# One MLP unit back from the Strassen form, attention's weighted sum as one strided reduction, and DVE work handed to GpSimd, in a two-layer attention and MLP kernel

## The chip, the cores and the metric

The kernel runs on one core of a Trainium2 chip. The metric is the device time in microseconds (us) of one execution. The engines are named as in the profile: PE is the matrix engine, DVE the vector engine, ACT the scalar engine, POOL is GpSimd, SP is the engine that issues most DMAs. Each engine runs its own queue of instructions in the order in which they were written, and waits at the head of its queue until what an instruction needs is there.

## The reference

Two layers follow each other twice on 2048 tokens of 640 numbers in fp32: sliding attention, then an MLP, each with a layernorm ahead and a residual sum behind.

```python
S, D, H, Dh, W, dil, F = 2048, 640, 32, 20, 8, 2, 1536
def A(x, wqkv, wo):
    q, k, v = heads(x @ wqkv)                     # 32 heads of 20
    # token s sees the tokens s, s-2, ..., s-14, those below 0 masked
    logits = einsum("bhsd,bhswd->bhsw", q, k[idx]) * Dh ** -0.5
    o = einsum("bhsw,bhswd->bhsd", softmax(logits), v[idx])
    return merge(o) @ wo
def B(y, w1, b1, w2, b2):
    return gelu(y @ w1 + b1) @ w2 + b2
for _ in range(2):
    x = x + A(layernorm(x), wqkv, wo)
    x = x + B(layernorm(x), w1, b1, w2, b2)
```

## The kernel before

The tokens of each parity are independent in attention, so the 2048 tokens are cut into four units of 512 (two parities, two halves), and the two layers make eight unit steps, numbered 0 to 7. In a unit each of the 128 partitions holds four consecutive tokens of its parity.

Matrix products are made in split form: a fp32 operand is written as a high and a low fp16 half, and three products (high with high, high with low, low with high) are summed, so a product over 640 takes 15 matmuls.

A unit step goes as follows. `layernorm` (ACT, with the power -0.5 on POOL, L487) writes y, its two halves and, by a DMA transpose, `yT`. `qkv` projects (L539), ACT evacuates to `ev`, and `put` stores q, k and v to a scratch tensor in HBM (`spill`), from ACT's queue. `fetch` loads them back with the seven tokens ahead of each partition's own. `attention` then works on one group of 8 heads (160 numbers per token) at a time, four groups per unit, 32 groups `G` in all. For each half of a group (two tokens per partition) DVE multiplies q by the eight shifted k (L606), sums over the 20 numbers of a head (L610), takes the softmax over 8 terms (L618 to L625; L618 and L623 reduce over the shifts, which lie 8 floats apart), multiplies by the shifted v (L632, into `pr`, laid out as token, shift, 160 numbers), and adds the eight shifts in three additions of halves: eight to four and four to two (L640), two to one (L644, into `o`). ACT writes the high half of `o` to `ohl`, DVE the low half (L653). `project` transposes `ohl` by DMA (4 times per unit) and multiplies by wo (L672); DVE adds to the residual x (L678).

A unit's plain MLP (`mlp`) runs 12 steps: 15 matmuls to 128 hidden columns (L709), gelu and high half on ACT (L715, L718), low half on DVE (L720), and 24 matmuls into the accumulators (L728, L731), at the end DVE's residuals (L751). For the units in `FAST_OUT`, `mlp_fast` does the second product in a Strassen-like form, with seven products in place of eight: sums of hidden blocks (L854, on POOL except for unit 7), their halves (L849) and 252 matmuls of 320 columns (L900). The weight sums for it are made by `prep_sums` (30 operations on POOL, L776) and kept in HBM. Behind the layernorm of the MLP, b2 is added to x (L515).

The order of all engines' queues is worked out ahead by `Plan`: every operation is added with an engine, an estimated duration and a priority; `run` simulates the engines and starts, at each point, the operation that can start first, ties by priority, with buffers taken from pools. The code is then written out in that order, so a queue's order is fixed before the kernel runs, and an operation that takes longer than estimated delays what stands behind it.

```python
for w in (4, 2):
    dve(EH * w * GC, G - 0.9, lambda vk=vk, w=w: nc.vector.tensor_add(
        tile_of(*vk)[:, :, 0:w], tile_of(*vk)[:, :, 0:w], tile_of(*vk)[:, :, w:2 * w]),
```

Of the kernel before, what the change touches and what calls it, by code (L numbers as in the profile page):

```python
# [15 lines left out]
P = 128  # L16
KD = D // P
NF = F // P
NG = 4
# [27 lines left out]
FAST_OUT = (6, 7)  # L47
# [16 lines left out]
class Plan:  # L64
# [12 lines left out]

    PATIENCE = 0.7
# [12 lines left out]
    def add(self, eng, dur, prio, emit, need=(), give=(), use=(), table=None, move=0.0, lazy=False):  # L91
        o = dict(eng=eng, dur=dur, prio=prio, emit=emit, need=need, give=give, use=use, table=table,
                 move=move, lazy=lazy, n=len(self.ops))
# [6 lines left out]
    def run(self):  # L100
# [13 lines left out]
        order = []  # L114

        def start(o):
# [3 lines left out]
            for k in o["need"]:  # L120
                e, w = when[k]
                w = w + (self.LAG[e] if e != o["eng"] else 0.06 * (e != "pe"))
                t = max(t, w)
            new = {}
            for u in o["use"]:
                if u in self.slot:
                    t = max(t, self.since[u])
                else:
# [7 lines left out]
                    new[u[0]] = i + 1  # L136
            return t

        total = len(self.ops)
        while len(order) < total:  # L140
# [19 lines left out]
            d = o["dur"]  # L160
            if o["table"] and o["table"] != table:
                table = o["table"]
                d += self.SWITCH
# [21 lines left out]
            for k in o["give"]:  # L185
                when[k] = (e, end)
# [19 lines left out]
def sliding_dilated_then_mlp_kernel(  # L206
# [76 lines left out]
    T["g"] = [b[:, :NS * HT2].rearrange("p (s c) -> p s c", s=NS) for b in (act_buf, ev_buf)]  # L283
# [27 lines left out]
    def dve(n, prio, emit, need=(), give=(), use=(), more=0.0):  # L311
        plan.add("dve", v_cost(n) + more, prio, emit, need, give, use)
# [3 lines left out]

    def dma(kb, prio, emit, need=(), give=(), use=(), by="sp"):
        lazy = give[0][0] in ("x", "sq", "st", "c1", "c2", "zero", "mw", "tr", "ms", "fw") or give[0] in ("b1", "b2")
        plan.add(by, 0.1 if by == "act" else 0.38, prio, emit, need, give, use, move=kb / 330.0, lazy=lazy)

    def dma_transpose(prio, emit, need=(), give=(), use=()):
        plan.add("sp", 1.45, prio, emit, need, give, use, move=1.4)
# [5 lines left out]
    def constants():  # L328
        nc.vector.memset(half, -0.5)
# [6 lines left out]
    def mask_value():  # L336
        nc.vector.tensor_scalar(mask, mask, 0.0, -1e9 / scale, op0=OP.is_lt, op1=OP.mult)
# [67 lines left out]
    def prep_m(f, i, prio):  # L405
# [4 lines left out]
        dma(328, prio - 5, lambda: nc.scalar.dma_start(mw[i][f], tile_of(*ck)),  # L410
            need=[("lo", ("m", f, i))], give=[("mw", f, i)], use=[ck], by="act")

    def turn(prio, t, name, hk, yk):

        for a in range(2):
# [10 lines left out]
            def copy(a=a, turned=turned):  # L426
                to = transposed(yk)[:, a * KD:(a + 1) * KD, t * P:(t + 1) * P]
                ps = turned().rearrange("p (k c) -> p k c", k=KD)
                if a:
                    nc.vector.tensor_copy(to, ps)  # L430
# [12 lines left out]
    def layernorm(n, prio, yk, twice):  # L443
# [13 lines left out]
        for t in range(m if fast else 0):  # L457
            def stats(t=t):
# [3 lines left out]
                nc.vector.tensor_scalar_add(bn[:, t, 13:14], bn[:, t, 13:14], EPS)  # L462
# [19 lines left out]
        for t0 in range(0, 0 if fast else m, cut):  # L482
# [4 lines left out]
            pool(2.5, prio, lambda t0=t0, t1=t1: nc.gpsimd.tensor_tensor(  # L487
# [6 lines left out]
        for t in range(m):  # L494
# [19 lines left out]
            if twice:  # L514
                dve(D, -350, lambda t=t: nc.vector.tensor_add(x[u][:, t], x[u][:, t], b2),  # L515
                    need=[("y", name, t), ("fg", n, 2, 0) if n in FAST_OUT else ("hhi", at(n, t) * NF + 2 * t + 2), "b2"], give=[("xb", n, t)])

# [3 lines left out]
    def qkv(n):  # L521
# [6 lines left out]
        for k, (g, b) in enumerate(halves):  # L528
            ek = ("ev", (n, g, b))
            for i in range(2):  # L530
# [12 lines left out]
                mm(3 * KD * 3 * GC, 15, -500 + n + 0.01 * k, product,  # L543
# [5 lines left out]
            def put(g=g, b=b, ek=ek):  # L549
                to = spill[la][par]  # L550
                nc.scalar.dma_start(
# [5 lines left out]
                give=[("put", n, g, b)], use=[ek], by="act")  # L557
# [20 lines left out]
    def attention(G):  # L578
# [21 lines left out]
        for a in range(NE):  # L600
# [3 lines left out]
            def qk(t0=t0, pk=pk):  # L604
                w = tile_of(*wk)
                nc.vector.tensor_mul(tile_of(*pk), w[:, HALO + m + t0:HALO + m + t0 + EH, None, :].to_broadcast([P, EH, W, GC]),  # L606
# [5 lines left out]
                axis=AX.X, op=OP.add), need=[("qk", G, a)], give=[("lg", G, a)], use=[pk, sk])  # L612
# [14 lines left out]
        for a in range(NE):  # L627
# [3 lines left out]
            def pv(t0=t0, vk=vk):  # L631
                nc.vector.tensor_mul(  # L632
# [5 lines left out]
            last = ("pv", G, a)  # L638
            for w in (4, 2):
                dve(EH * w * GC, G - 0.9, lambda vk=vk, w=w: nc.vector.tensor_add(  # L640
                    tile_of(*vk)[:, :, 0:w], tile_of(*vk)[:, :, 0:w], tile_of(*vk)[:, :, w:2 * w]),
                    need=[last], give=[("ad", G, a, w)], use=[vk])
                last = ("ad", G, a, w)
# [356 lines left out]
```

## Time and profile before

| what | value |
|---|---|
| median of 2 runs | 1189.59 us (1188.9 to 1190.28) |
| the profiled execution's own time | 1189.57 us |
| its span | 1187.8 us |
| mean granted clock of PE | 0.99 |
| last attention result written | 1052.47 us |

The span runs from the first to the last instruction; the execution's time is 1.8 us longer. A group's row in the profile names line, engine, operation, the program's tensors, the shape (partitions x elements) and the count, then busy time and mean duration of one, then the time its engine sat idle just before.

### The profile page before, as it was taken

What the parts mean: (1) busy time and instruction counts of PE and PEld (TensorE: products, weight loads), DVE (VectorE), ACT (ScalarE), POOL (GpSimd) and SP (SyncE); (2) the same over time, 40 slices, a digit from 0 to 9 for tenths busy, and PEclk for the clock granted to TensorE, in tenths of its full rate; (3) what the DMA queues carried; (4) which work ended last, traced back from release to release, by engine and by line L of the source; (5) the groups of instructions that cost most, each with busy time, mean ns of one, the idle gap of its engine ahead of it and who ended that gap; (6) DMA issues with size and microseconds to landing.
All of it is one profiled execution on the core that took longest, in us unless ns stands there. A gap on an engine that the chain in (4) does not pass through costs nothing.

```text
span 1187.8 us, 17373 instructions
## 1 busy us (share of the span) xinstructions
PE 1153.7 (97%) x6844; PEld 632.0 (53%) x6844; DVE 1063.6 (90%) x1030; ACT 538.3 (45%) x939; POOL 153.0 (13%) x100
## 2 busy tenths in 40 slices
PE   7999999999979999999999999999998799989998
PEld 4444446577544565545554455546454555447556
DVE  7899999999999999999998999989999999873361
ACT  6476444535283435732637253364343552344240
POOL 1011000001010000000002010022055440450000
PEclk9999999999999999999999999999999899989999
DMA  9998999889675558577565757568766894546645
GB/s 303 289 314 271 309 328 279 244 264 289 172 218 161 175 170 205 164 195 207 153 199 150 203 152 210 182 159 175 212 237 238 231 241 130 183 100 187 182 124 173
DMA packets 235758, 248.77 MB, mean 209 GB/s; under 512 B 131148, under 2 KB 185756, under 8 KB 235676
## 3 DMA queue, kind: packets, MB, share of 16 engines
q1 hardware_dynamic: 206620, 208.34, 61.5%
q10 hardware_dynamic: 29056, 39.33, 9.5%
q8 instruction: 53, 0.87, 0.3%
q14 instruction: 29, 0.24, 0.1%
HBM read 168.76 MB, written 48.71 MB: 183 GB/s over the span
## 4 chain that ended last, share of the span: by engine, by line
PE 66%; DVE 21%; issue 6%; POOL 3%; ACT 2%; DMA 2%; SPq 0%; DVEq 0%; POOLq 0%; ACTq 0%
PE ps L539 25%; PE ps L709 12%; PE acc L728 9%; PE ps L672 8%; PE acc L900 6%; DVE pr L606 4%; DVE pr L632 4%; PE ps L834 3%; DVE pr L640 3%; DVE sm L610 3%; PE acc L731 2%; POOL ln L487 2%; DVE act L720 2%; DVE xf L515 1%; DVE hl L506 1%
## 5 line engine op out<-in xcount | busy, mean ns | idle before, releaser
L539 PE MATMUL ps<-wq,yT 128*128 128x480 f16 x1920 | 392.6, 367 | 0.0
L539 PEld LDWEIGHTS <-yT 128*128 128x128 f16 x1920 | 187.9, 98 | 201.2 <-issue 1.5
L709 PE MATMUL ps<-yT,c 128*128 128x512 f16 (+1 forms) x1260 | 248.8, 351 | 6.4 <-DMA yT<-hl 6.4
L728 PE MATMUL acc<-c,act 128*128 128x512 f16 x864 | 240.4, 379 | 2.4 <-DVE act L720 2.3
L632 DVE TENSOR_TENSOR pr<-sm,v 128x2560 f32<-128x2560 f32 x64 | 182.4, 2868 | 0.0
L709 PEld LDWEIGHTS <-c 128*128 128x128 f16 x1260 | 120.7, 98 | 114.7 <-issue 9.9
L606 DVE TENSOR_TENSOR pr<-qk 128x2560 f32<-128x2560 f32 x64 | 179.6, 2807 | 0.1
L610 DVE TENSOR_REDUCE sm<-pr 128x128 f32<-128x2560 f32 x64 | 179.6, 2806 | 0.0
L731 PE MATMUL acc<-c,act 128*128 128x128 f16 x864 | 178.6, 219 | 0.9 <-DVE act L720 0.9
L487 POOL TENSOR_TENSOR ln<-ln,half 128x2 f32<-128x2 f32 (+1 forms) x30 | 58.2, 1938 | 761.1 <-ACT ln L484 761.1
L672 PE MATMUL ps<-wo,yT 128*128 128x320 f16 x960 | 136.7, 305 | 14.2 <-DMA yT<-ohl 12.4
L545 ACT ACTIVATE ev<-ps 128x480 f32<-128x480 f32 x128 | 72.3, 566 | 170.3 <-PE ps L539 169.9
L640 DVE TENSOR_TENSOR pr<-pr 128x640 f32<-128x640 f32 (+1 forms) x128 | 148.7, 1184 | 0.0
L728 PEld LDWEIGHTS <-act 128*128 128x128 f16 x864 | 84.2, 98 | 101.0 <-DVE act L720 3.7
L672 PEld LDWEIGHTS <-yT 128*128 128x128 f16 x960 | 95.4, 100 | 55.9 <-DMA yT<-ohl 14.2
L715 ACT ACTIVATE act<-ps,b 128x512 f32<-128x512 f32 (+1 forms) x84 | 52.1, 623 | 156.4 <-PE ps L709 148.1
L731 PEld LDWEIGHTS <-act 128*128 128x128 f16 x864 | 82.0, 98 | 8.9 <-DVE act L720 1.0
L834 PE MATMUL ps<-yT,c 128*128 128x512 f16 x360 | 78.5, 379 | 0.4 <-ACT act L840 0.3
L470 ACT ACTIVATE junk<-xf 128x640 f16<-128x640 f32 x56 | 41.2, 735 | 81.6 <-DVE xf L678 71.4
L720 DVE TENSOR_TENSOR act<-act 128x512 f16<-128x512 f32 (+1 forms) x84 | 58.0, 693 | 15.2 <-ACT act L718 15.1
L776 POOL TENSOR_TENSOR wq<-wq 128x320 f32<-128x320 f32 (+1 forms) x30 | 56.4, 1898 | 67.8 <-ACT wq L798 47.4
L900 PE MATMUL acc<-c,wq 128*128 128x320 f16 x420 | 61.8, 299 | 0.0
(82 smaller groups left out, 942.0 us busy)
## 6 DMA issues: line engine op xcount, KB each, us to landing
c<-mw SPq DMA_DIRECT2D x192, 320.0 KB, 3.4
spill<-ev ACTq DMA_DIRECT2D x64, 480.0 KB, 4.2
qk<-spill SPq DMA_DIRECT2D x32, 880.0 KB, 6.2
v<-spill SPq DMA_DIRECT2D x32, 880.0 KB, 4.9
qk<-spill SPq DMA_DIRECT2D x32, 320.0 KB, 4.0
mw<-c ACTq DMA_DIRECT2D x24, 320.0 KB, 4.7
c<-msp SPq DMA_DIRECT2D x24, 320.0 KB, 3.5
act<-in_B_w_dram SPq DMA_DIRECT2D x21, 320.0 KB, 5.6
```

The lines of the kernel that those rows point to most:

```text
L487: pool(2.5, prio, lambda t0=t0, t1=t1: nc.gpsimd.tensor_tensor(col(2)[:, t0:t1], col(2)[:, t0:t1], half[:, t0:t1], op=OP.pow), need=[("vr" ...
L539: nc.tensor.matmul(ps, transposed(yk)[:, a * KD + k, t * P:(t + 1) * P], wq[:, b, k, g], start=j == 0, stop=j == 3 * KD - 1)
L606: nc.vector.tensor_mul(tile_of(*pk), w[:, HALO + m + t0:HALO + m + t0 + EH, None, :].to_broadcast([P, EH, W, GC]), windows(w, t0, [GC, W], ...
L610: dve(E, G - 0.7, lambda pk=pk, t0=t0: nc.vector.tensor_reduce(lg(t0, t0 + EH).rearrange("p t w h -> p (t w h)"), tile_of(*pk).rearrange(" ...
L632: nc.vector.tensor_mul(tile_of(*vk).rearrange("p t w (h d) -> p t (w h) d", d=DH), lg(t0, t0 + EH).rearrange("p t w h -> p t (w h)")[:, :, ...
L640: dve(EH * w * GC, G - 0.9, lambda vk=vk, w=w: nc.vector.tensor_add(tile_of(*vk)[:, :, 0:w], tile_of(*vk)[:, :, 0:w], tile_of(*vk)[:, :, w ...
L672: nc.tensor.matmul(tile_of(*pk)[:, :D // 2], transposed(yk)[:, a * KD + k, t * P:(t + 1) * P], wo[:, b, k, c * D // 2:(c + 1) * D // 2], s ...
L709: nc.tensor.matmul(tile_of(*pk)[:, :nt], tile_of(*ck)[:, a, k * P:(k + 1) * P], transposed(yk)[:, c * KD + k, t0 * P:t1 * P], start=i == 0 ...
L728: nc.tensor.matmul(acc[i], w, tile_of(*wk)[:, c, :BANK], start=e == 0 and (a, c) == PASS[0], stop=end, skip_group_check=True)
L731: nc.tensor.matmul(acc[4][:, i * P:(i + 1) * P], w, tile_of(*wk)[:, c, BANK:], start=e == 0 and i == t0 and (a, c) == PASS[0], stop=end, s ...
L834: nc.tensor.matmul(tile_of(*pk), tile_of(*ck)[:, a, k * P:(k + 1) * P], transposed(yk)[:, c * KD + k, :], start=i == 0, stop=i == 3 * KD - 1)
L900: nc.tensor.matmul(acc[bank][:, :HD], tile_of(*hk)[half][:, a, slot, t * P:(t + 1) * P], load()[:, z, c], start=q in FIRST and i == 0 and ...
```

## The change

It has several parts.

- `FAST_OUT` goes from (6, 7) to (7,): unit 6's MLP is computed in plain form, unit 7's keeps the Strassen form. The two buffers of the Strassen form's sums change places, and their wait for the unit ahead moves from its first to its second step.
- Attention's three additions become one `tensor_reduce` that reads `pr` with the shift as innermost dimension, 160 floats from term to term, and writes `o`.
- The low half of `o` (three groups of four) and the addition of b2 (units 0 to 6) are done by POOL (`laid`). A DVE operation can be marked with `opens`; while it runs, a window is open in the plan in which such a POOL operation can be placed. The POOL operation is then made to wait for the DVE instruction ahead of the one that opens the window.
- `prep_sums` moves from POOL to DVE, at a low priority.
- The stores of q, k and v and of the split MLP weights go from ACT's queue to SP's.
- The plan adds spare time (0.5 us for a DMA, 2.0 for a transpose) to what PE waits for from DMA, and counts 3.0 instead of 2.5 us for the power on POOL. Unit 4's projection gets a later priority.

```diff
-FAST_OUT = (6, 7)
+SPARE = (0.5, 2.0)
+FAST_OUT = (7,)
...
+        def window(o, t):
+            for w in windows:
+                if o["beside"] > w[3]:
+                    continue
+                s = max(t, w[0])
+                if s + o["dur"] <= w[1] + self.OVER:
+                    return s, w
+            return None, None
...
-                e, w = when[k]
-                w = w + (self.LAG[e] if e != o["eng"] else 0.06 * (e != "pe"))
+                e, w, spare = when[k]
+                w = w + (self.LAG[e] if e != o["eng"] else 0.06 * (e != "pe")) + spare * (o["eng"] == "pe")
...
-    T["g"] = [b[:, :NS * HT2].rearrange("p (s c) -> p s c", s=NS) for b in (act_buf, ev_buf)]
+    T["g"] = [b[:, :NS * HT2].rearrange("p (s c) -> p s c", s=NS) for b in (ev_buf, act_buf)]
...
+    def laid(n, prio, emit, until, need=(), give=(), use=(), level=1):
+        plan.add("pool", 0.17 + n / 450.0, prio, emit, need, give, use, beside=level, until=until)
...
-                dve(D, -350, lambda t=t: nc.vector.tensor_add(x[u][:, t], x[u][:, t], b2),
-                    need=[("y", name, t), ("fg", n, 2, 0) if n in FAST_OUT else ("hhi", at(n, t) * NF + 2 * t + 2), "b2"], give=[("xb", n, t)])
+                last = lambda by, t=t: by.tensor_tensor(x[u][:, t], x[u][:, t], b2, op=OP.add)
+                if n in FAST_OUT:
+                    dve(D, -350, lambda last=last: last(nc.vector), need=[("y", name, t), ("fg", n, 2, 0), "b2"], give=[("xb", n, t)])
+                else:
+                    laid(D, -250 + n, lambda last=last: last(nc.gpsimd), lambda ready, when, k=("rest", n, PARTS[at(n, t)][1]): k in when, need=[("y", name, t), "b2"], give=[("xb", n, t)], level=2)
...
-                nc.scalar.dma_start(
+                nc.sync.dma_start(
...
-            last = ("pv", G, a)
-            for w in (4, 2):
-                dve(EH * w * GC, G - 0.9, lambda vk=vk, w=w: nc.vector.tensor_add(
-                    tile_of(*vk)[:, :, 0:w], tile_of(*vk)[:, :, 0:w], tile_of(*vk)[:, :, w:2 * w]),
-                    need=[last], give=[("ad", G, a, w)], use=[vk])
-                last = ("ad", G, a, w)
-            dve(EH * GC, G - 0.9, lambda vk=vk, t0=t0: nc.vector.tensor_add(
-                tile_of(*ok)[:, t0:t0 + EH], tile_of(*vk)[:, :, 0], tile_of(*vk)[:, :, 1]),
-                need=[last], give=[("o", G, a)], use=[vk, ok])
+            dve(E, G - 0.9, lambda vk=vk, t0=t0: nc.vector.tensor_reduce(
+                tile_of(*ok)[:, t0:t0 + EH], tile_of(*vk).rearrange("p t w c -> p t c w"), axis=AX.X, op=OP.add),
+                need=[("pv", G, a)], give=[("o", G, a)], use=[vk, ok], opens=2)
...
+        low = lambda by: by.tensor_tensor(tile_of(*hk)[:, :, 1, g * GC:(g + 1) * GC], tile_of(*ok), hi(), op=OP.subtract)
+        if g < NG - 1:
+            laid(m * GC, -300 + G, lambda: low(nc.gpsimd), lambda ready, when: any(("o", G + 1) in q["use"] for q in ready.get("dve", ())), need=[("oh", G)], give=[("ol", G)], use=[ok, hk])
+        else:
+            dve(m * GC, -300 + G, lambda: low(nc.vector), need=[("oh", G)], give=[("ol", G)], use=[ok, hk])
...
-            pool(1.0, prio, f, need=need, give=[("ts", j, name)], use=[key])
+            dve(HD, prio, f, need=need, give=[("ts", j, name)], use=[key])
...
+        if o["behind"]:
+            tc.add_manual_dep(o["ins"].ins, o["behind"]["ins"].ins.name, mybir.DependencyInfo(
+                mybir.DependencyClass.Sync, mybir.DependencyReason.DATA), reason="order")
```

The order of the queues changes throughout. At the end of the last attention group DVE's queue stands like this before (`pr` holds the weighted values, `o` the sums, `wq` the halves of unit 6's Strassen sums; a number behind a name is the buffer's):

```order
L640 TENSOR_TENSOR pr_74<-pr_74 128x2x640
L640 TENSOR_TENSOR pr_75<-pr_75 128x2x640
L849 TENSOR_TENSOR wq<-ev,wq 128x768
L849 TENSOR_TENSOR wq<-ev,wq 128x1024
L515 TENSOR_TENSOR xf<-xf,b_103 128x640 x4
L849 TENSOR_TENSOR wq<-act,wq 128x768
L849 TENSOR_TENSOR wq<-act,wq 128x1024
L640 TENSOR_TENSOR pr_74<-pr_74 128x2x320
L640 TENSOR_TENSOR pr_75<-pr_75 128x2x320
L644 TENSOR_TENSOR o_86<-pr_74 128x320
L644 TENSOR_TENSOR o_86<-pr_75 128x320
L653 TENSOR_TENSOR ohl_73<-o_86,ohl_73 128x4x160
```

And like this now, with L668 the product, L674 the reduction, L753 the low half of the plain MLP and L809 the weight sums:

```order
L668 TENSOR_TENSOR pr_75<-sm_88,v_69 128x2560
L753 TENSOR_TENSOR act<-act 128x512
L674 TENSOR_REDUCE o_86<-pr_75 128x320
L753 TENSOR_TENSOR act<-act 128x512
L668 TENSOR_TENSOR pr_74<-sm_88,v_69 128x2560
L809 TENSOR_TENSOR wq<-wq 128x4x320
L753 TENSOR_TENSOR act<-act 128x512
L674 TENSOR_REDUCE o_86<-pr_74 128x320
L809 TENSOR_TENSOR wq<-wq 128x4x320
L683 TENSOR_TENSOR ohl_73<-o_86,ohl_73 128x4x160
```

The six additions have become two reductions, b2 and the Strassen halves have left this place, and one weight sum has come ahead of the last reduction.

On PE, at the last matmul of the last output projection (`wo` is its weight), this followed before:

```order
L672 LDWEIGHTS yT_72
L672 MATMUL ps_94<-wo,yT_72 128x320
L900 LDWEIGHTS wq
L900 MATMUL acc_95<-c_76,wq 128x320
L900 LDWEIGHTS wq
```

Now this follows, with L705 the projection and L761 and L764 the plain MLP's second product:

```order
L705 MATMUL ps_94<-wo,yT_71 128x320
L761 LDWEIGHTS act
L761 MATMUL acc_97<-c_79,act 128x512
L764 LDWEIGHTS act
L764 MATMUL acc_99<-c_79,act 128x128
```

Where unit 6's 252 Strassen products stood behind the projection, 407 matmuls of unit 6's plain MLP stand now, ahead of unit 7's MLP in both.

POOL's queue early in the program held nothing but the powers of the layernorms (`ln`), after those of the first two (`bn`):

```order
L465 TENSOR_TENSOR bn<-bn,half 128x1 x8
L487 TENSOR_TENSOR ln_91<-ln_91,half 128x2 x2
L487 TENSOR_TENSOR ln_89<-ln_89,half 128x2 x2
L487 TENSOR_TENSOR ln_90<-ln_90,half 128x1 x4
L487 TENSOR_TENSOR ln_91<-ln_91,half 128x2
```

Now the low halves (L683) and the additions of b2 (L548, on `xf`) stand between them:

```order
L498 TENSOR_TENSOR bn<-bn,half 128x1 x8
L520 TENSOR_TENSOR ln_91<-ln_91,half 128x2 x2
L520 TENSOR_TENSOR ln_89<-ln_89,half 128x2 x2
L683 TENSOR_TENSOR ohl_73<-o_86,ohl_73 128x4x160 x3
L520 TENSOR_TENSOR ln_90<-ln_90,half 128x1 x4
L548 TENSOR_TENSOR xf<-xf,b_103 128x640
L683 TENSOR_TENSOR ohl_73<-o_86,ohl_73 128x4x160
```

A power that stands behind one of these waits until it has run.

More of the change, by code (lines that the diff above doesn't have):

```diff
@@ L114, in run @@
         order = []
+        windows = []
+        shut = sum(o["opens"] > 0 for o in self.ops)
+        ahead = None
+        def window(o, t):
[6 more added lines that the diff above has]
+            return None, None
         def start(o):
@@ L136, in start @@
                     new[u[0]] = i + 1
+            if o["beside"] and (shut or windows):
+                s, _ = window(o, t)
+                return s if s is not None or shut and not o["until"](ready, when) else t
             return t
@@ L185, in run @@
             for k in o["give"]:
-                when[k] = (e, end)
+                when[k] = (e, end, o["spare"])
                 for w in waiting.pop(k, ()):
@@ L328, in constants @@
     def constants():
[L329 removed]
+        return nc.vector.memset(half, -0.5)
     dve(8, -900, constants, give=["half"])
@@ L823, in mlp_fast @@
             gk, hk = ("g", (b, jj)), ("h", (b, jj))
+            if jj == 1:
+                free += [("out", b - 1, NF - 1, i) for i in range(M)]
             for s in range(2):
```

80 lines of the change are left out of this document (45 added, 35 removed).

## The prediction

> **What bounds the kernel now.** I read the page's busy shares and slices first, then the table of stretches, then the groups of VectorE (DVE) by shape, and last the chain of waits near the end.
>
> ```profile
> span 1187.8 us, 17373 instructions
> PE 1153.7 (97%) x6844; PEld 632.0 (53%) x6844; DVE 1063.6 (90%) x1030; ACT 538.3 (45%) x939; POOL 153.0 (13%) x100
> PE   7999999999979999999999999999998799989998
> DVE  7899999999999999999998999989999999873361
> ```
>
> Two engines are nearly full. PE is full to the end; DVE is full for some 34 of 40 slices and falls off when attention is over. So the table of stretches is cut where the last attention result is written (1052.47 us), and, in a second answer, into pieces of the time before.
>
> ```profile
> 0.00:1052.47 1052.47, 1026.12 (x6035) 552.21 (x6036) 1009.66 (x943) 498.09 (x876) 143.99 (x90) 0.99 0.73 215
> 1052.47:1057.62 5.15, 1.26 (x6) 0.39 (x5) 4.35 (x4) 3.79 (x5) 2.63 (x3) 0.84 0.49 93
> 1057.62:1187.80 130.18, 126.36 (x804) 79.44 (x804) 49.62 (x84) 36.42 (x58) 6.40 (x8) 0.98 0.59 166
> ...
> 0.00:15.00 15.00, 10.01 (x91) 7.24 (x92) 8.56 (x21) 5.22 (x6) 2.15 (x11) 0.89 0.94 295
> 15.00:100.00 85.00, 84.04 (x436) 41.18 (x434) 78.42 (x91) 56.09 (x111) 13.08 (x10) 1.00 0.92 285
> 800.00:900.00 100.00, 98.58 (x571) 52.20 (x570) 99.45 (x82) 42.03 (x71) 30.86 (x17) 1.00 0.72 202
> 900.00:1000.00 100.00, 91.30 (x558) 49.44 (x557) 100.00 (x88) 47.64 (x73) 35.22 (x18) 0.97 0.77 229
> ```
>
> The columns are the stretch, its length, then busy time of PE, weight load, DVE, ACT and POOL. Up to the last attention result DVE is busy 1009.7 of 1052.5 us: it idles 42.8 us, 13.0 of them in the first 100 us, and between 800 and 1000 us 0.6 us, while PE idles 10. From there to the end stand 5.15 us of storing and transposing and 130.2 us in which PE has 126.4 us of work. So the end is the time of the last attention result, set by DVE's sum, plus the PE work that stands in PE's order behind the last output projection. DVE had no more than about 30 us to spare after the start. An edit that adds to attention on DVE shows almost fully; one that takes from it soon meets PE.
>
> **The strided sum.** These are DVE's groups by shape (busy us, mean ns of one):
>
> ```profile
> L610 DVE TENSOR_REDUCE sm<-pr 128x128 f32<-128x2560 f32 x64 | 179.6, 2806 | 0.0
> L640 DVE TENSOR_TENSOR pr<-pr 128x1280 f32<-128x1280 f32 x64 | 96.4, 1521 | 0.0
> L640 DVE TENSOR_TENSOR pr<-pr 128x640 f32<-128x640 f32 x64 | 53.5, 846 | 0.0
> L720 DVE TENSOR_TENSOR act<-act 128x512 f16<-128x512 f32 x60 | 48.2, 804 | 14.0 <-ACT act L718 13.9
> L644 DVE TENSOR_TENSOR o<-pr 128x320 f32<-128x320 f32 x64 | 32.7, 521 | 0.0
> L515 DVE TENSOR_TENSOR xf<-xf,b 128x640 f32<-128x640 f32 x32 | 29.2, 925 | 0.0
> L653 DVE TENSOR_TENSOR ohl<-o,ohl 128x640 f16<-128x640 f32 x32 | 27.6, 862 | 3.0 <-ACT ohl L651 3.0
> L618 DVE TENSOR_REDUCE sm<-sm 128x32 f32<-128x256 f32 x32 | 19.5, 608 | 0.0
> L751 DVE SCALAR_TENSOR_TENSOR xf<-acc,xf 128x512 f32<-128x512 f32 x29 | 18.3, 681 | 1.0 <-PE acc L731 0.9
> L619 DVE TENSOR_TENSOR sm<-sm 128x256 f32<-128x256 f32 x32 | 13.3, 416 | 0.0
> L849 DVE TENSOR_TENSOR wq<-act,wq 128x1024 f16<-128x1024 f32 x6 | 7.3, 1223 | 5.5 <-ACT wq L851 5.5
> ```
>
> Consecutive operations overlap a little, so the timeline gives the step from start to start:
>
> ```profile
> 110.16 1.47 DVE L640 TENSOR_TENSOR pr<-pr 128x1280 f32<-128x1280 f32 x1
> 111.56 2.81 DVE L632 TENSOR_TENSOR pr<-sm,v 128x2560 f32<-128x2560 f32 x1
> ...
> 119.80 0.61 DVE L618 TENSOR_REDUCE sm<-sm 128x32 f32<-128x256 f32 x1
> 120.33 2.81 DVE L606 TENSOR_TENSOR pr<-qk 128x2560 f32<-128x2560 f32 x1
> ```
>
> The 1.47 us addition is followed after 1.40: a step is its duration less 0.07. The three additions cost (1.521+0.846+0.521) - 3*0.07 = 2.68 us, 64 times 171.4 us. In their place stand 64 reductions over 2560 elements, whose price R is not in the trace. At the low end, L610 reduces 2560 elements that lie side by side: 2.74 us a step. But the new one reads its eight terms 640 bytes apart (160 floats). The trace has one reduction that reads with a gap: L618 takes groups of eight terms 32 bytes apart, and 256 elements cost 608 ns where L619 passes 256 in 416. The excess, 192 ns, is 0.75 ns per element, so 2560 elements would take 2.74 + 1.92 = 4.66 us. Read by its step, 0.53 us for 256, ten times as many cost 5.3; by its full duration, 6.08 - 0.07 = 6.0. L618 is the nearest row, in kind of operation, group length and gap, so I stay with it, between its first two readings: R = 5.0, with 2.74 and 6.0 as far ends. The additions were 171.4; the reductions are 320.
>
> The Trainium skill says otherwise in "VectorE: DVE Perf Modes", Mode 1x (REGULAR): one result per cycle with no assumption on the pattern ("fp32, weird strides, PSUM operands — all work"). By that rule the sum would be near that of L610, the first rival below. The L618 row speaks against it; another page, "SBUF — State Buffer", Door 1: The DMA port swizzle, has each access that enters a new 16-byte line pay a penalty, which agrees with L618's excess and would scale it by the element.
>
> **What leaves and joins DVE before the last attention result.** The low halves of the attention output go to POOL for three groups in four: 24 x (0.862-0.07) = 19.0 us off. Adding b2 goes to POOL for units 0 to 6: 28 x (0.925-0.07) = 23.9 off. Unit 6 in plain form takes six splittings of L849 away (6 x 1.15 = 6.9), five residuals of L751 (5 x 0.61 = 3.1) move behind the last result and one more L720 (0.7) ahead of it: 9.3 off. Of the 30 weight sums that come from POOL, eight of 320 and one of 1280 elements stand ahead: 8 x 0.45 + 1.45 = 5.1 on. Together, without R: -171.4 - 19.0 - 23.9 - 9.3 + 5.1 = -218.5. With 64 x 5.0 = 320 DVE gains 101.5 us of work, and has 1111.2 ahead of the last result.
>
> **POOL.** What it takes over is priced by its uncontended runs:
>
> ```profile
> 861.47 3.45 POOL L776 TENSOR_TENSOR wq<-wq 128x320 f32<-128x320 f32 x4 [31.50 <-ACT wq L798]
> 873.64 5.79 POOL L776 TENSOR_TENSOR wq<-wq 128x320 f32<-128x320 f32 x4 [2.34 <-ACT wq L798]
> 961.85 2.62 POOL L776 TENSOR_TENSOR wq<-wq 128x1280 f16<-128x1280 f32 x1 [1.38 <-ACT wq L803]
> ```
>
> 0.86 us for 320 elements and 2.62 for 1280 give 1.45 for 640; 52 of them are 75 us on an engine that is 13% busy and sheds the weight sums. I cost them at nothing; what hides them is the long reductions, behind whose predecessor each is made to wait. If that cover goes, they cost DVE up to 75 (second rival). Behind each stand POOL's layernorm powers, and behind those PE; with DVE setting the pace PE has room.
>
> **PE.** The chain of waits shows the prices:
>
> ```profile
> 394.76 3.24 PE ps L709 x15
> 401.26 3.24 PE ps L709 x15
> ...
> 1057.62 18.98 PE ps L672 x120
> ...
> 1149.76 34.24 PE acc L900 x252
> ```
>
> A step of the plain MLP takes 6.50 us and a unit twelve: 78.0. The Strassen form takes 12 x 3.24 + 34.24 = 73.1. PE's sum grows by 4.9 us. Of more weight is the order: behind the last projection PE had unit 6's 252 Strassen products and unit 7, and now has 407 of unit 6's plain matmuls (39 to a step, so 10.4 steps, 67.8 us) and unit 7. The end lies 5.15 + 130.2 - 34.2 + 67.8 = 168.9 us behind the last attention result, against 135.3.
>
> **Queues.** 64 stores of q, k, v and 24 of split weights go from ACT's queue to SP's, behind what SP waits for:
>
> ```profile
> spill<-ev ACTq DMA_DIRECT2D x64, 480.0 KB, 4.2
> mw<-c ACTq DMA_DIRECT2D x24, 320.0 KB, 4.7
> ...
> SPq L570 <- DVE pr L632: 137.7, 26, 11.0
> ```
>
> SP's longest such wait is 11.0 us. Unit 0's stores come before any such wait and later units are projected well ahead, so I take nothing, at most 11, and see no gain over 4.2 x 2 at the start. Unit 4's later projection and the swapped buffers only reorder PE work with slack: nothing, within the idle time below.
>
> **The sum.** DVE's idle time before the last result was 42.8 us: 13.0 at the start stays; of the rest I keep half (800 to 1000 us shows that it vanishes where DVE binds), 28 in all, ends 13 and 43. 1111.2 + 28 + 168.9 = 1308.1 us of span. The profiled run took 1189.57 us, 1.8 over its span, and the median of the runs is 1189.59: 1310. With R from 4.66 to 5.3 and idle time from 13 to 43 this goes from 1273 to 1344.
>
> **Rivals.** *The gap costs nothing on DVE* (R = 2.74, or an excess per instruction: 2.93). DVE's path is then 1009.7 - 43.1 + 28 + 168.9 + 1.8 = 1165, and PE decides: 1189.6 + 4.9 = 1194.5, less what it waited for and may no longer:
>
> ```profile
> PE ps L672 <- DMA yT<-ohl: 12.4, 3, 6.8
> PE ps L709 <- DMA yT<-hl: 6.4, 1, 6.4
> ```
>
> That is 1176 to 1195; 1187 within 2%. It ends on the other side. For it speaks L610; against it L618. It decides as long as R stays under 2.74 + (1213.4-1165)/64 = 3.5 us. *POOL blocks DVE*: R small, but the 52 moved operations each hold up DVE for 1.45: 1165 + 75 = 1240. For it: the same four POOL operations took 3.45 and 5.79 us, and L515 averages 925 ns where L640's form of 640 elements takes 846. Against it: each starts behind a named instruction ahead of a reduction. It needs 33 of 52 to pass 2%. *The gap costs more than L618's*: R = 6.0 gives 1374.
>
> **Chances.** The forecast (R 4.4 to 5.6) 0.72; the gap free 0.18; POOL blocking or an R between 0.05; R over 5.6 0.05. Of the free case 0.02 is faster by over 2% and 0.16 within; of the 0.05 for POOL or an R between, 0.01 falls within too. So faster 0.02, same 0.17, slower 0.81; 2% (24 us) is about what a measurement of this kernel can tell from no change. The likeliest case's own range is 1273 to 1344. To leave out no more than 2 in 10 the range must reach into the free case: 1183 to 1345.
>
> **What would show it.** Right: reductions onto `o` with a mean near 5 us in the by-shape groups; DVE at 97% or more to about 1140 us; PE waiting before every output projection for transposes of `ohl`, and its share down near 89%; the last projection to the end about 164 us. Wrong: a mean under 3.5 us, which would leave PE the bound with one more plain unit (sum up 5 us); POOL operations much over 1.5 us with DVE operations stretched beside them; DVE with more than 45 us idle before the last attention result, which would mean that a wait on POOL's or SP's queue has joined.

## The result, and the profile after

The changed kernel takes 1252.64 us (two runs, 1252.46 to 1252.82) against 1189.59: a ratio of 1.0527, 95% interval 1.0502 to 1.0553. It is slower, inside the range that was given and 57 us under the forecast of 1310. These lines of the page after the change answer to those shown of before (the last is from the chain that ended last):

```profile
span 1251.0 us, 17351 instructions
PE 1174.4 (94%) x6880; PEld 634.9 (51%) x6880; DVE 1136.3 (91%) x871; ACT 531.3 (42%) x939; POOL 119.9 (10%) x98
PE   8999989799999979989998989979998999799998
DVE  7999999999999999999999999999999999843271
DVE 50%; PE 30%; issue 14%; DMA 3%; ACT 2%; SPq 0%; DVEq 0%
```

In the kernel before, that chain read:

```profile
PE 66%; DVE 21%; issue 6%; POOL 3%; ACT 2%; DMA 2%; SPq 0%; DVEq 0%; POOLq 0%; ACTq 0%
```

PE's share of the span has fallen from 97 to 94%, DVE's row of slices is full for as long as attention lasts, and the chain has passed from PE to DVE. The table of stretches, cut again at the last attention result (1084.34 us) and at the start of the last projection, has the same columns as before: stretch, length, busy time of PE, weight load, DVE, ACT and POOL.

```profile
0.00:1084.34 1084.34, 1015.10 (x5905) 545.18 (x5906) 1068.61 (x763) 474.06 (x854) 117.84 (x96) 0.98 0.67 200
1084.34:1092.12 7.78, 3.85 (x19) 1.86 (x18) 6.33 (x10) 3.15 (x5) 0.00 (x0) 0.78 0.68 173
1092.12:1251.00 158.88, 155.46 (x959) 87.89 (x957) 61.37 (x100) 54.08 (x80) 2.03 (x2) 1.00 0.62 174
```

Ahead of the last attention result DVE is busy 1068.6 of 1084.3 us and idle 15.7, where it was busy 1009.7 and idle 42.8. So 58.9 us more of work made that result 31.9 us late, and 166.7 us follow it instead of 135.3. The groups by shape show the new reduction, two other groups of DVE, and POOL's new operations:

```profile
L674 DVE TENSOR_REDUCE o<-pr 128x320 f32<-128x2560 f32 x64 | 293.8, 4601 | 0.0
L668 DVE TENSOR_TENSOR pr<-sm,v 128x2560 f32<-128x2560 f32 x64 | 179.9, 2824 | 0.1
L753 DVE TENSOR_TENSOR act<-act 128x512 f16<-128x512 f32 x72 | 49.9, 693 | 26.1 <-ACT act L751 26.1
L548 POOL TENSOR_TENSOR xf<-xf,b 128x640 f32<-128x640 f32 x28 | 43.3, 1547 | 155.2 <-DVE act L753 35.7 <-DVE pr L668 22.4 <-DVE xf L711 19.4
L683 POOL TENSOR_TENSOR ohl<-o,ohl 128x640 f16<-128x640 f32 x24 | 36.3, 1512 | 334.4 <-DVE sm L659 104.4 <-DVE sm L655 93.6 <-DVE sm L661 25.1
```

The reduction takes 4.60 us, where one over adjacent floats took 2.81. POOL's operations take 1.5 us, and DVE's are not longer than before: L668 is L632 of before, 2868 ns then, and L753 is L720, 804 ns then.

### The profile page after: what moved, and what is told of

It is laid out like the page before. It is cut to its first block, busy times and chain, and to the rows that moved or that the text cites. A ratio compares the mean times of both kernels' runs of the same rounds, so it can differ in the third digit from the quotient of the medians.

```text
span 1251.0 us, 17351 instructions
## 1 busy us (share of the span) xinstructions
PE 1174.4 (94%) x6880; PEld 634.9 (51%) x6880; DVE 1136.3 (91%) x871; ACT 531.3 (42%) x939; POOL 119.9 (10%) x98
## 4 chain that ended last, share of the span: by engine, by line
DVE 50%; PE 30%; issue 14%; DMA 3%; ACT 2%; SPq 0%; DVEq 0%
DVE o L674 14%; DVE pr L642 9%; PE ps L742 8%; PE acc L761 8%; DVE pr L668 8%; DVE sm L646 7%; PE ps L705 4%; PE ps L868 3%; PE acc L934 3%; DVE hl L539 3%; PE acc L764 2%; DMA yT<-hl 2%; DVE act L753 1%; PE ps L575 1%; DVE xf L711 1%
## 5 line engine op out<-in xcount | busy, mean ns | idle before, releaser
L575 PE MATMUL ps<-wq,yT 128*128 128x480 f16 x1920 | 395.8, 368 | 13.5 <-ACT ev L581 10.6
L761 PE MATMUL acc<-c,act 128*128 128x512 f16 x1008 | 288.5, 387 | 25.7 <-DVE xf L784 14.0
L674 DVE TENSOR_REDUCE o<-pr 128x320 f32<-128x2560 f32 x64 | 293.8, 4601 | 0.0
L742 PE MATMUL ps<-yT,c 128*128 128x512 f16 (+1 forms) x1440 | 287.7, 353 | 0.0
L764 PE MATMUL acc<-c,act 128*128 128x128 f16 x1008 | 210.8, 222 | 3.6 <-DVE xf L784 1.9
L742 PEld LDWEIGHTS <-c 128*128 128x128 f16 x1440 | 137.9, 98 | 127.0 <-issue 0.3
L668 DVE TENSOR_TENSOR pr<-sm,v 128x2560 f32<-128x2560 f32 x64 | 179.9, 2824 | 0.1
L761 PEld LDWEIGHTS <-act 128*128 128x128 f16 x1008 | 99.7, 99 | 135.0 <-issue 10.1
L705 PE MATMUL ps<-wo,yT 128*128 128x320 f16 x960 | 141.9, 311 | 25.4 <-DVE xf L711 14.8
L705 PEld LDWEIGHTS <-yT 128*128 128x128 f16 x960 | 97.0, 101 | 70.0 <-issue 16.4
L764 PEld LDWEIGHTS <-act 128*128 128x128 f16 x1008 | 97.1, 99 | 25.5 <-issue 15.0
L681 ACT ACTIVATE ohl<-o 128x640 f16<-128x640 f32 x32 | 23.6, 737 | 193.8 <-DVE o L674 193.8
L753 DVE TENSOR_TENSOR act<-act 128x512 f16<-128x512 f32 (+1 forms) x96 | 59.6, 623 | 27.3 <-ACT act L751 27.3
L520 POOL TENSOR_TENSOR ln<-ln,half 128x2 f32<-128x2 f32 (+1 forms) x30 | 33.5, 1116 | 477.9 <-ACT ln L517 477.9
L683 POOL TENSOR_TENSOR ohl<-o,ohl 128x640 f16<-128x640 f32 x24 | 36.3, 1512 | 334.4 <-DVE sm L659 104.4
L548 POOL TENSOR_TENSOR xf<-xf,b 128x640 f32<-128x640 f32 x28 | 43.3, 1547 | 155.2 <-DVE act L753 35.7
```

What stands on the lines that cost most here:

```text
L575: nc.tensor.matmul(ps, transposed(yk)[:, a * KD + k, t * P:(t + 1) * P], wq[:, b, k, g], start=j == 0, stop=j == 3 * KD - 1)
L668: return nc.vector.tensor_mul(tile_of(*vk).rearrange("p t w (h d) -> p t (w h) d", d=DH), lg(t0, t0 + EH).rearrange("p t w h -> p t (w h)" ...
L674: dve(E, G - 0.9, lambda vk=vk, t0=t0: nc.vector.tensor_reduce(tile_of(*ok)[:, t0:t0 + EH], tile_of(*vk).rearrange("p t w c -> p t c w"), ...
L705: nc.tensor.matmul(tile_of(*pk)[:, :D // 2], transposed(yk)[:, a * KD + k, t * P:(t + 1) * P], wo[:, b, k, c * D // 2:(c + 1) * D // 2], s ...
L742: nc.tensor.matmul(tile_of(*pk)[:, :nt], tile_of(*ck)[:, a, k * P:(k + 1) * P], transposed(yk)[:, c * KD + k, t0 * P:t1 * P], start=i == 0 ...
L753: dve(nt, -1000, lambda h32=h32, hk=hk: nc.vector.tensor_sub(tile_of(*hk)[:, 1, :nt], tile_of(*h32)[:, :nt], tile_of(*hk)[:, 0, :nt]), nee ...
```

## The experiments

Theory G: the gap of 640 bytes sets the reduction's price, and DVE's sum the time. Its first rival, Q, has the stores on SP's queue and POOL's work hold things up. Each time stands against runs of the kernel before on the same chip.

**The same kernel, reading adjacent floats.** Nothing but the read pattern differs; the reduction then adds other terms, so this run serves for its time alone.

```diff
-tile_of(*vk).rearrange("p t w c -> p t c w")
+tile_of(*vk).rearrange("p t w c -> p t (w c)").rearrange("p t (c w) -> p t c w", w=W)
```

> The changed kernel with one thing altered: the reduction reads eight adjacent floats where it read eight 640 bytes apart, so it sums other terms; every queue keeps its order. Theory G (the gap sets the price of the reduction, and DVE's sum sets the time): the reduction falls from 4.60 us to about 2.8, DVE sheds 64 x 1.8 = 115 us, PE becomes the bound, 1180 to 1197 us. Rival Q (stores on SP's queue and work on POOL hold things up): it stays above 1220. Rival S (the sum is dear for its 320 outputs of short groups, not for the gap): the reduction stays near 4.6 us and the time near 1250.

Measured: 1161.41 us, ratio 0.9762 (0.9743 to 0.9780). Its page's first rows and the reduction's group:

```profile
span 1160.8 us, 17351 instructions
PE 1150.2 (99%) x6880; PEld 628.8 (54%) x6880; DVE 1025.9 (88%) x871; ACT 535.7 (46%) x939; POOL 112.8 (10%) x98
...
L674 DVE TENSOR_REDUCE o<-pr 128x320 f32<-128x2560 f32 x64 | 179.2, 2809 | 0.0
```

With every queue in the same order, the reduction falls to 2.81 us and the time by 91 us. The gap is shown to be the cause, and Q and S fall. The time is below what G allowed, though: without the gap the change would be 28 us faster than the kernel before.

**The additions back.** The three additions of the kernel before stand in place of the reduction, with all else of the change.

```diff
-            dve(E, G - 0.9, lambda vk=vk, t0=t0: nc.vector.tensor_reduce(
...
+            for w in (4, 2):
+                dve(EH * w * GC, G - 0.9, lambda vk=vk, w=w: nc.vector.tensor_add(
...
```

> The changed kernel with the three additions back in place of the reduction, all other parts kept. Theory G: DVE sheds 64 x (4.49 - 2.68) = 116 us, PE is the bound with one more plain unit, 1180 to 1197 us. Rival Q: above 1220. If POOL's work then blocks the two-input additions, DVE operations of L640's kind grow by 0.1 us or more beside POOL's, and the time comes to 1200 to 1220.

Measured: 1162.40 us, ratio 0.9773 (0.9758 to 0.9788), a version that beats both kernels and, like the last run, lies below G's range. POOL's work beside the additions costs little: the time stays far under the 1200 us of the last branch. PE is the bound here:

```profile
PE 1151.0 (99%) x6880; PEld 629.1 (54%) x6880; DVE 1017.2 (88%) x999; ACT 534.5 (46%) x939; POOL 131.8 (11%) x98
```

**The reduction alone, in the kernel before.**

```diff
-            for w in (4, 2):
-                dve(EH * w * GC, G - 0.9, lambda vk=vk, w=w: nc.vector.tensor_add(
...
+            dve(E, G - 0.9, lambda vk=vk, t0=t0: nc.vector.tensor_reduce(
...
```

> The kernel before with the strided reduction in place of the three additions, and no other part of the change. Theory G: DVE gains 64 x (4.49 - 2.68) = 116 us ahead of the last attention result, which had 43 us of idle time of which about 16 stay, so that result comes near 1142 to 1150 us, and 113 us behind it make 1255 to 1270. Rival Q: the reduction alone costs little, under 1220.

Measured: 1284.56 us, ratio 1.0799 (1.0780 to 1.0818), above G's range. The reduction takes 4585 ns and DVE is busy 1136.5 of 1160.7 us ahead of the last attention result, 126.8 more than before and not 116: the plan has put other work there too. 122.9 us follow, not 113. So the reduction costs 95 us here, and the rest of the change is worth 32 us to a kernel that is bound by DVE.

**The measured price in the plan.** The instructions are those of the change; the plan counts 1.76 us more for each reduction and lays the queues out for it.

```diff
-                need=[("pv", G, a)], give=[("o", G, a)], use=[vk, ok], opens=2)
+                need=[("pv", G, a)], give=[("o", G, a)], use=[vk, ok], opens=2, more=1.76)
```

> The changed kernel, with the reduction entered into the plan at 1.76 us more (4.49), so that the queues are laid out for its measured price; the instructions are the same. Behind the last projection PE then has 432 matmuls (73 us by columns) in place of 839 (139). Theory O (half of the loss is the order: PE waits through attention and has too much left at its end): the last attention result comes some 15 to 25 us later, since more of DVE's MLP work stands ahead, and the end 100 us behind it: 1203 to 1215 us. Theory D (DVE's sum alone sets the time, whatever the order): within 10 us of 1252.

Measured: 1233.30 us, ratio 1.0366 (1.0348 to 1.0385). The stretches, cut at the last attention result, and PE's longest waits:

```profile
0.00:1110.44 1110.44, 1067.07 (x6328) 576.01 (x6328) 1083.48 (x784) 496.91 (x877) 116.32 (x96) 0.98 0.69 205
1110.44:1232.00 121.56, 94.50 (x552) 55.25 (x552) 53.70 (x88) 41.80 (x62) 1.99 (x2) 0.87 0.55 149
...
PE ps L742 <- DMA yT<-hl: 28.0, 2, 22.6
PE ps L868 <- DMA yT<-hl: 17.8, 1, 17.8
PE ps L705 <- DMA yT<-ohl: 11.6, 1, 11.6
```

The last result comes 26 us later, about as O has it, and 121.6 us follow it, not 100: with little MLP work left behind the last projection, PE now waits 17.8 us for unit 7's layernorm and transposes (second row of the waits). So 19 of the 63 us lay in an order laid out for too low a price. That is less than O's half, and more than the 10 us that D allowed. What bounds this run is less clear than before. DVE is still busy 1083.5 of the 1110.4 us ahead of the last attention result, but the chain that ended last runs mostly over PE:

```profile
PE 86%; DVE 7%; DMA 3%; issue 1%; ACT 1%; SPq 0%; ACTq 0%; DVEq 0%
```

How the other 44 us divide between DVE's sum and PE's waits for transposes is not shown.

**The price of a gap, by itself.** A probe of single reductions and additions over the same 2560 floats:

```python
def gap(t, s, w, n=N):   # groups of w terms, s floats apart
    return t[:, :n].rearrange("p (b w s) -> p b s w", w=w, s=s)
nc.vector.tensor_reduce(res(s, w, n), gap(src, s, w, n), axis=AX.X, op=OP.add)
```

> A probe: reductions and additions on DVE alone, six times each, with nothing of the reference computed but a copy of x. Groups of eight over the same 2560 floats, read 1, 2, 4, 8, 16, 40 and 160 floats apart; groups of 2, 4, 16 and 20; 256 and 1280 elements; additions that read or write with a gap of 160 floats. Theory L (each read that enters a new 16-byte piece costs more): 2.8 us for gaps of 1 and 2 floats, 4.6 us for 4, 8, 16, 40 and 160 alike, and for groups of 2 to 20 alike with a gap; an addition that reads with the gap 4.6 too. Theory T (short groups cost, whatever the gap): gap 1 in groups of eight costs near 4.6 too, groups of 20 near 2.8 with or without a gap. Theory F (the price grows with the distance): 8 floats near 2.8 to 3.0, 160 floats 4.6.

The groups by shape, in the order of the table below them (mean ns in the column before the last):

```profile
L38 DVE TENSOR_REDUCE dst<-src 128x320 f32<-128x2560 f32 x6 | 16.9, 2810 | 0.2
L39 DVE TENSOR_REDUCE dst<-src 128x320 f32<-128x2560 f32 x6 | 16.9, 2820 | 0.2
L40 DVE TENSOR_REDUCE dst<-src 128x320 f32<-128x2560 f32 x6 | 28.1, 4682 | 0.2
L41 DVE TENSOR_REDUCE dst<-src 128x320 f32<-128x2560 f32 x6 | 28.4, 4727 | 0.2
L42 DVE TENSOR_REDUCE dst<-src 128x320 f32<-128x2560 f32 x6 | 26.5, 4419 | 0.2
L43 DVE TENSOR_REDUCE dst<-src 128x320 f32<-128x2560 f32 x6 | 30.5, 5076 | 0.2
L44 DVE TENSOR_REDUCE dst<-src 128x320 f32<-128x2560 f32 x6 | 26.7, 4452 | 0.2
L47 DVE TENSOR_REDUCE dst<-src 128x128 f32<-128x2560 f32 x6 | 26.6, 4431 | 0.2
L53 DVE TENSOR_REDUCE dst<-src 128x640 f32<-128x2560 f32 x6 | 26.9, 4484 | 0.2
L54 DVE TENSOR_REDUCE dst<-src 128x1280 f32<-128x2560 f32 x6 | 17.1, 2848 | 0.2
L48 DVE TENSOR_REDUCE dst<-src 128x32 f32<-128x256 f32 x6 | 3.6, 608 | 0.2
L57 DVE TENSOR_TENSOR dst<-src,two 128x2560 f32<-128x2560 f32 x6 | 16.9, 2825 | 0.2
L58 DVE TENSOR_TENSOR dst<-src,two 128x2560 f32<-128x2560 f32 x6 | 27.2, 4528 | 0.2
L56 DVE TENSOR_TENSOR dst<-src,two 128x2560 f32<-128x2560 f32 x6 | 27.3, 4549 | 0.2
```

| line | what is read or written with a gap | gap, floats | terms in a group |
|---|---|---|---|
| 38, 39 | sum reads | 1, 2 | 8 |
| 40, 41, 42, 43, 44 | sum reads | 4, 8, 16, 40, 160 | 8 |
| 47 | sum reads | 128 | 20 |
| 53, 54 | sum reads | 640, 1280 | 4, 2 |
| 48 | sum of 256 elements reads | 8 | 8 |
| 57 | addition, nothing with a gap | 1 | - |
| 58, 56 | addition writes; addition reads one operand | 160 | - |

Theory L holds but for one row and some spread: a gap of 8 bytes is free, and with the gaps of 16 bytes and more each element costs 0.63 to 0.89 ns extra ((4419-2810)/2560 to (5076-2810)/2560), with no trend in the distance or the length of the group, and for an addition as for a sum, in reading as in writing. T and F fall: groups of eight without a gap cost 2.81, and 160 floats less than 8. But groups of two terms 5120 bytes apart cost nothing extra (L54), against L's expectation. L48 repeats, to the nanosecond, the 608 ns of the kernel's own L618. The kernel's reduction reads as L44 does but takes 4.60 us, 0.15 more than the probe's 4.45; what adds this is not shown (over adjacent floats both take 2.81). Laying `pr` out so that the reduction reads adjacent floats would move the gap into the write of the multiplication, which L58 suggests would cost about the same; that was not run.

**Where the other 28 us come from.** The next runs start from the additions (1162 us) and undo one more part, or put one part alone into the kernel before.

Strassen form in both units again:

```diff
-FAST_OUT = (7,)
+FAST_OUT = (6, 7)
...
-            if jj == 1:
+            if jj == 1 and b - 1 not in FAST_OUT:
```

> The changed kernel with the three additions back and Strassen form in units 6 and 7, as before the change, so that what is left of the change is POOL's work, the weight sums on DVE, the queues and the plan. Theory P (PE is the bound once the reduction is gone): PE has 4.9 us less to do than in the run with the additions alone (1162): 1155 to 1160 us. If the form costs nothing since PE hides it: 1162. If its sums on DVE and POOL cost more than they save: above 1165.

Measured: 1174.08 us, 0.9872 (0.9857 to 0.9888): dearer by 12 where 5 less was expected. PE's sum did fall, but one wait came:

```profile
PE ps L874 <- ACT ev L880: 15.1, 1, 15.1
```

PE waits until ACT has evacuated unit 6's first hidden block into `ev`. By the chain that ended last, that evacuation stands in ACT's queue (1029.96 us) right behind weight sums of `prep_sums` (1025.54 and 1028.70 us), whose raw weights landed only at 1025.5. So most of the wait comes from a clash of two parts: the weight sums have a low priority now, and with unit 6 in Strassen form the plan needs them a unit sooner. The swap of the buffers, another candidate, was not tried by itself.

POOL's new work back on DVE, as in the kernel before:

```diff
-        if g < NG - 1:
+        if False:
             laid(m * GC, -300 + G, lambda: low(nc.gpsimd), lambda ready, when: any(("o", G + 1) in q["use"] for q in ready.get("dve", ())), need=[("oh", G)], give=[("ol", G)], use=[ok, hk])
...
-                if n in FAST_OUT:
-                    dve(D, -350, lambda last=last: last(nc.vector), need=[("y", name, t), ("fg", n, 2, 0), "b2"], give=[("xb", n, t)])
...
+                dve(D, -350, lambda t=t: nc.vector.tensor_add(x[u][:, t], x[u][:, t], b2),
...
```

> The changed kernel with the three additions back, and the low halves and b2 back on DVE. Theory P2 (the 28 us that the other parts won come from DVE's 43 us less, which takes PE's waits away): DVE has as much ahead of the last attention result as in the kernel before, and the time comes back to 1178 to 1195 us. Rival Q2 (they come from the stores' queue or the plan's spare times): it stays at 1160 to 1168.

Measured: 1165.58 us, 0.9801 (0.9785 to 0.9816). DVE takes 32 us more (1049.3 us busy against 1017.2) and the time 3. P2 falls: DVE had that much to spare. The time is in Q2's range; the next three runs take the queue and the spare times by themselves.

Stores back on ACT's queue:

```diff
-                nc.sync.dma_start(
+                nc.scalar.dma_start(
...
-                give=[("put", n, g, b)], use=[ek])
+                give=[("put", n, g, b)], use=[ek], by="act")
```

> The changed kernel with the three additions back, and the stores of q, k, v and of the split weights on ACT's queue as before. Theory P2: no difference that matters, 1158 to 1167 us. Rival Q2 (the queue is what won): 1175 or more.

Measured: 1168.15 us, 0.9823 (0.9806 to 0.9841): 6 us, between the two expectations.

The plan's spare times alone, in the kernel before:

```diff
-                w = w + (self.LAG[e] if e != o["eng"] else 0.06 * (e != "pe"))
+                w = w + (self.LAG[e] if e != o["eng"] else 0.06 * (e != "pe")) + spare * (o["eng"] == "pe")
```

> The kernel before with one part of the change: the plan counts 0.5 us more for a DMA and 2.0 more for a DMA transpose where PE waits for it. Theory S (the spare times won the 28 us, since PE waited for transposes before): PE's waits for yT, 18.8 us in the kernel before, are nearly gone, and the time is 1160 to 1172 us. Rival W (they came from less work on DVE, POOL and queues together): 1183 to 1195.

Measured: 1181.37 us, 0.9941 (0.9926 to 0.9956), 7 us faster than the kernel before on the same chip, between S and W. PE no longer waits for `ohl`'s transposes, but once 10.4 us for a residual. And almost without spare times, beside the additions:

```diff
-SPARE = (0.5, 2.0)
+SPARE = (0.0, 0.3)
```

> The changed kernel with the three additions back and spare times of 0.0 and 0.3 us in place of 0.5 and 2.0 (with none at all the plan finds no order). Theory S: PE waits for transposes again, 1175 to 1195 us. Rival W: 1160 to 1168, as with the additions alone (1162).

Measured: 1163.36 us, 0.9785 (0.9769 to 0.9800). Beside the other parts the spare times are worth nothing: S falls.

Three parts undone at once, on top of the additions (the edits of the runs with both units in Strassen form, without POOL's work and with stores on ACT):

> The changed kernel with the three additions, Strassen form in units 6 and 7, POOL's new work back on DVE and the stores back on ACT's queue; what is left of the change is the spare times, the weight sums on DVE and unit 4's later projection. The three parts undone cost 12, 3 and 6 us one by one: 1183 us if they add up. Theory S: 1170 to 1183, below the kernel before by what the spare times give. Rival W: 1185 to 1195.

Measured: 1213.01 us, 1.0212 (1.0195 to 1.0229), outside both expectations and slower than the kernel before: 51 us more than with the additions alone, where the single costs add to 21 us. Here too one wait stands out:

```profile
PE ps L708 <- ACT ev L877: 38.7, 1, 38.7
```

It is now the last projection that waits for a buffer, but behind the same evacuation as in the run with both units in Strassen form, and over twice as long. The chain that ended last leads through the weight sums again:

```profile
1023.38 3.58 DMA wq<-in_B_w_dram
1026.99 1.28 ACT wq L834
...
1039.60 4.92 DMA wq<-in_B_w_dram
1044.62 1.28 ACT wq L834
...
1049.11 1.27 ACT wq L839
1050.37 0.58 ACT ev L877
1051.00 18.30 PE ps L708 x120
```

L834 scales the raw weights that the DMA brings, L839 writes the sums' halves, and only then comes the evacuation (L877). The parts do not add up, and this clash is a large part of why: the kernel before had these sums on POOL, at a higher priority. A run with both units in Strassen form and the weight sums earlier was not made.

The plain unit 6 alone, in the kernel before:

```diff
-FAST_OUT = (6, 7)
+FAST_OUT = (7,)
```

> The kernel before with one part of the change: unit 6's MLP in plain form. Theory P (PE pays 4.9 us more and nothing else moves): 1190 to 1196 us. Rival V (the plain form takes the sums on POOL and their halves on DVE out of the stretch of attention where DVE was full, so the last attention result comes 10 to 20 us earlier and PE's waits of 900 to 1060 us go): 1168 to 1182.

Measured: 1188.84 us, 0.9987 (0.9977 to 0.9998): no difference that matters, a little under P. By itself this part neither wins nor loses.

## Why the prediction was right, and where its sizes were off

**What bounds the kernel, and the direction: right.** DVE's sum up to the last attention result plus the PE work behind the last projection gives the time after, as it gave it before: 1068.6 + 15.7 + 166.7 = 1251.0 us of span. The run with adjacent floats shows the gap to be the cause, and the run with the reduction alone that it needs no other part. The size was less good. The sum's own range was 1273 to 1344 us, and 1252.64 lies below it; it is inside the stated range only because that was stretched down to 1183 for the rival without a gap. Four terms were too high or took off too little, all on the same side: the price of the reduction (33 us), what leaves DVE (10), the idle time (12) and the tail (2).

**The price R: right in kind, 0.5 us too high.** The step was forecast at 5.0 us, between two readings of L618, and is 4.49 by the timeline of the changed kernel, where a multiplication follows a reduction:

```profile
1048.15 4.61 DVE L674 TENSOR_REDUCE o<-pr 128x320 f32<-128x2560 f32 x1
1052.64 2.85 DVE L668 TENSOR_TENSOR pr<-sm,v 128x2560 f32<-128x2560 f32 x1
```

Of the two readings, the excess per element (4.66) was the nearer; the reading by the whole step counted L618's own fixed time ten times. This is the largest term that was mis-sized: 64 x 0.51 = 33 of the 57 us. The rule of the Trainium skill, "VectorE: DVE Perf Modes", Mode 1x (REGULAR), that strides need no assumption, does not hold for the rate here: the probe has 4.45 us with a gap of 160 floats and 2.81 without. The rule of the Trainium skill, "SBUF — State Buffer", Door 1: The DMA port swizzle, that an access to a new 16-byte line pays, agrees with the threshold of the probe (8 bytes free, 16 not), though not with its row of two terms (2.85 us).

**What leaves and joins DVE: 10 us too little.** Without R the sum fell by 228 us, not 218.5 (1068.6 - 1009.7 - 64 x 4.49 = -228.5). The multiplications and L753 became shorter, by 64 x 0.044 and some 60 x 0.11 us, about 9 together. The trace of the kernel before shows why, in two places beside the same kind of POOL operation:

```profile
867.15 4.16 POOL L776 TENSOR_TENSOR wq<-wq 128x1280 f16<-128x1280 f32 x1 [2.23 <-ACT wq L803]
868.75 5.23 DVE L632 TENSOR_TENSOR pr<-sm,v 128x2560 f32<-128x2560 f32 x1
...
899.34 2.81 DVE L610 TENSOR_REDUCE sm<-pr 128x128 f32<-128x2560 f32 x1
899.91 2.62 POOL L776 TENSOR_TENSOR wq<-wq 128x1280 f16<-128x1280 f32 x1 [1.38 <-ACT wq L803]
```

Beside a DVE operation with two inputs both are stretched: L632 takes 5.23 us where it takes 2.81 without POOL, and POOL's operation 4.16 instead of 2.62. Beside a reduction neither is. Over the whole trace DVE's operations with two inputs run some 24 us beyond the medians of their groups before the change and 1 us after it. So the prediction's 925 ns for L515 and its prices of the additions held some of this. POOL's new work is laid beside reductions.

**The idle time: 15.7 us, forecast 28.** The first 100 us keep 9.7 of it (DVE is busy 90.3 us in them); where DVE binds, next to nothing is left, as the rows of 800 to 1000 us before the change had shown. The low end was the one to take.

**The tail: right**, 166.7 against 168.9. **POOL: right in price** (1.5 us against 1.45). Its cover held: no group of DVE grew by more than 0.03 us. **Queues: right** that the stores cost nothing on SP; beside the additions they even save the 6 us that the run with stores on ACT lost.

**The signs for PE: wrong.** PE was to wait before every output projection for transposes of `ohl`, with its share near 89%. Its share is 94%, partly since PE was busy 20.7 us longer, and its waits at the projections are these:

```profile
PE ps L705 <- DVE xf L711: 14.8, 8, 3.2
PE ps L705 <- DMA yT<-ohl: 6.2, 1, 6.2
```

One projection waited for a transpose; eight times, 14.8 us together, PE waited for DVE to add a projection's result to the residual and free its buffer. DVE sets the pace, but through the buffers as well as through the results.

**The rival without a gap: its mechanism right, its size wrong.** It was given 1176 to 1195 us and measured 1161. I let PE win back only two waits, 18.8 us, and took less than half of them. The page of before held more: PE was idle for 34.1 us of the span (1187.8 - 1153.7), against 10.6 in the run with adjacent floats. That is 23.5 us. Its busy time fell as well, by 3.5 us, in spite of 4.9 us more work; the two are the 27 us of span. The mean granted clock was 0.998 there and 0.990 before, but the clock alone does not explain the busy time: for the same 6844 matmuls as before, PE was busy 1148.4 us at 0.980 in the run with three parts undone. No one part of the change gives the 27 us. Undone one by one each costs 1 to 12 us, put in alone the spare times give 7 and the plain unit 1. How much each of weight sums, unit 4's order and the rest contributes stays open, as runs for it were not made.

**What I did not price: the order.** Queues laid out for a reduction of 2.73 us leave too much for PE behind the last projection. The sum had that tail in it, 33.6 us more than before, but did not ask what part of the loss another order would return. It is 19 us by the run with the measured price.

## What to carry to other kernels

Where an engine's row has a shape with a gap, compare it with a row of the same count without one, and scale the excess by the element: that comparison alone held the sign and most of the size of this change. Three instructions made into one save little: in the probe 256 adjacent elements take 419 ns and 2560 take 2810, which leaves some 0.15 us of an instruction that does not go with the count, and the rate at which the one reads can cost many times that. And a bound engine that is 97% busy still has its idle time to give back: here 27 us, most of it idle time, which several parts returned together and none alone. Where one part is undone, look in the trace for what it collides with before its cost is put down to the part itself: with the second Strassen unit PE waited mostly for weight sums that came late.

## What the runs showed of the hardware that was not expected

- DVE reads or writes fp32 at 1.73 to 1.98 ns per element (4.42 and 5.08 us for 2560) with the gaps of 16 to 2560 bytes that were tried, and with 8 bytes at full rate (2.82 us). The dearest gap was 160 bytes, and 640 bytes were cheaper than 32 (4.45 against 4.73 us).
- Two streams 5120 bytes apart, read in turn, cost no more than one (2.85 us); four 2560 bytes apart did (4.48 us).
- A DVE operation with two inputs and a POOL operation stretch each other where they overlap (L632 5.23 us against 2.81 without POOL); a DVE reduction and a POOL operation do not (2.81 us, with POOL and without).
- PE's mean granted clock goes with its idle time: 0.969 to 0.978 in the three kernels in which PE idles longest (70 to 106 us), 0.998 to 0.999 where it idles 9 to 14. Its busy time for the same 6844 matmuls does not follow it: 1177.9 us at 0.969 with the reduction alone, but 1148.4 at 0.980 with three parts undone and 1153.7 at 0.990 in the kernel before.
